# Sparse attention and a squared-ReLU layer in one kernel: the arrival of s, b, w_out and one band of v, the first fillers, and new priorities of the planner

## The chip, the cores and the metric

The kernel runs on one core of a Trainium2 chip. A core has TensorE (PE in the profile, with its weight loads as PEld), VectorE (DVE), ScalarE (ACT), GpSimd (POOL) and SyncE (SP), which issues transfers. Sixteen DMA engines move data between the memory of the chip and the core's on-chip memory. The metric is the time on the device in microseconds. Lower is better.

## The reference

Eight batches of eight heads with 576 positions and 64 channels go through attention with fixed masks, and the result goes through a layer with a squared ReLU.

```python
scores = q @ k.T / 8                                # per batch and head, 576 x 576
mask_local   = (rel >= 0) & (rel < 32)              # heads 0 to 3; rel = query - key
mask_strided = (rel >= 0) & (key % 32 == query % 32)  # heads 4 to 7
attn = softmax(where(mask, scores, -1e9)) @ v
x = attn, heads side by side                        # 4608 x 512
h = x @ w_in                                        # 512 x 2048
g = s * relu(h) ** 2 + b                            # s and b are single numbers
out = g @ w_out                                     # 2048 x 512, float32
```

## The kernel before

**Attention.** A batch is done in four pairs of heads: m = 0 and 1 are the local pairs, m = 2 and 3 the strided ones. `pair_steps` makes the steps of a pair: transposes of q and k on TensorE (line 439 for the local pairs of batches 0 and 1, line 447 for others; later batches use DMA transposes), scores (line 568, with the mask added by line 565 in batch 0), exp on ScalarE (line 586), the product with v ("av", line 629), reciprocal and multiplication (lines 646 and 656) into `x_nat`, and the transpose to `xT` (line 676). The local pairs read v from `v_loc`, which has 128 partitions: a band of 96 positions and the 32 positions before it. `rows_before` copies these 32 rows on chip after the band has landed.

**The layer.** The 4608 tokens are cut into nine blocks T of 512. F1 is x @ w_in (`ff1`, line 928; line 1153 for the last two blocks), with a ReLU on ScalarE (line 954) or VectorE (line 956) and a square. F2 is g @ w_out (`ff2`, line 1183, for blocks 0 and 1; line 896 for later ones). From block 2 on, F2 is done with seven products in place of eight, and combinations of w_out (`w_mix`) and of g are added up on VectorE. The factor s and the term b come in at the end: F2's evacuation is out = s * psum + bcs (line 1194, or lines 815 and 827), where `bcs` is b times the column sums of w_out, made once by `bcs_steps` (lines 1210, 1221, 1228).

**What sets the order.** The class `Plan` holds a clock in ns. Every step on TensorE is a `Step` with a duration, needs, perhaps a PSUM bank, and "posts": work on other engines that it sets off. The main loop at the end of the kernel emits, at each time of this clock, an attention step, an F1 step or an F2 step whose needs are met, F1 before F2. The order in which steps are emitted is the fixed order of TensorE's instructions. Landings of transfers are assumed: `landing(cost)` adds the costs of transfers in the order of their requests, from a starting point `ring`. A step is therefore placed by assumed times, and on the chip TensorE waits at it if the data come later. `Plan.flush` chooses among posted work for ScalarE and VectorE: the smallest ready time plus an allowance from the table `LATER`, by the kind of the work; `SLACK` says how far ahead of the clock an engine may be given work.

While nothing is ready and fewer than 16 F1 steps have been emitted, `keep_running` emits fillers: matmuls of ones into a free bank (line 1431). The clock starts at 1850.

**The requests.** GpSimd asks for most loads,[...] in this order: q and k of batch 0, half of its band v, its strided v; then w_in in four parts (line 339); then, by `second`, q and k of batch 1 (lines 302 and 317), its band v (`load_vl`, line 322), its strided v (`early_v`), and w_out in four parts (line 345); then batch 2. SyncE asks for the identity, the other half of batch 0's band, the masks and, at lines 1311 and 1312, for s and b, each read from one number and spread over 128 partitions by the transfer:

```python
nc.sync.dma_start(out=s_sb, in_=moe_s.to_broadcast([128, 1]))
nc.sync.dma_start(out=b_sb, in_=moe_b.to_broadcast([128, 1]))
```

Of the kernel before, what the change touches and what calls it, by code (L numbers as in the profile page):

```python
# [1 line left out]

# [1 line left out]

# [7 lines left out]
FP32 = mybir.dt.float32  # L12
# [4 lines left out]
class Plan:  # L17
# [6 lines left out]

    LAT = {"A": 70.0, "V": 70.0, "P": 70.0, "D": 12000.0, "X": 7000.0, "Y": 12000.0}

    SLACK = 800.0
    LATER = {"g": 1500.0, "S": 1500.0, "in": 2500.0, "w_mix": 2500.0, "wc": 1500.0}

    def __init__(self):  # L30
        self.t = 0.0
        self.done = {}
        self.pend = []
        self.free = {"A": 0.0, "V": 0.0, "P": 7000.0, "D": 0.0, "X": 0.0, "Y": 0.0}
        self.banks = {}
# [85 lines left out]
        self.keys, self.posts, self.after = keys, posts, after  # L121


@with_exitstack
def kernel(
    ctx: ExitStack,
# [7 lines left out]
    moe_b: bass.AP,  # L134
    out: bass.AP,
):
    nc = tc.nc
    B, H, S, D = q.shape
    NTOK, DM = out.shape
    DFF = moe_w_in.shape[1]  # L140
    stride = 32
    scale = 1.0 / float(np.sqrt(D))
    PS = 512
# [40 lines left out]
    ident = const.tile([128, 128], FP16)  # L184
    masks = const.tile([128, LQ + SQ], FP16)
    mask_loc, mask_str = masks[:, 0:LQ], masks[0:SQ, LQ:LQ + SQ]
    s_sb = const.tile([128, 1], FP32)
    b_sb = const.tile([128, 1], FP32)

    w_in_sb = [const.tile([128, 4, n], FP16, name=f"w_in_sb{i}")  # L190
               for i, n in enumerate((512, 512, 512, 512))]
# [37 lines left out]
    x_dram = [tc.dram_tile([S, 128], FP16, name=f"x_dram{i}") for i in range(4)]  # L229

    sched = ctx.enter_context(tc.manual_schedule())
    plan = Plan()

# [100 lines left out]
    def load_w_in():  # L336
        wv = moe_w_in.rearrange("(c p) f -> p c f", p=128)
        for i, at in enumerate((0, 512, 1024, 1536)):
            nc.gpsimd.dma_start(out=w_in_sb[i], in_=wv[:, :, at:at + w_in_sb[i].shape[2]])

    def load_w_out(chunks):

# [76 lines left out]
    def pair_steps(b, m):  # L419
# [135 lines left out]
        def score(i, group):  # L555

            g, n = i // per_s, min(per_s, nt - i // per_s * per_s)

            def f():
                if i % per_s == 0:  # L560
                    st["s", g] = bank(group)
                c = i % per_s * 2 * nq
                if b < PE_MASK:

                    nc.tensor.matmul(
                        out=st["s", g][0:nk, c:c + 2 * nq], lhsT=ident[0:nk, 0:nk],
                        rhs=neg_loc if loc else neg_str, start=True, stop=False)
                nc.tensor.matmul(  # L568
                    out=st["s", g][0:nk, c:c + 2 * nq], lhsT=(st["k"][:, i * nq:i * nq + nk] if loc else st["k"][:, i, 0:SQ]),
                    rhs=st["q"][:, i].rearrange("d e c -> d (e c)"), start=b >= PE_MASK, stop=True)  # L570

            s = Step(f, (2 if b < PE_MASK else 1) * (2 * nq / 2.4 + 8), needs=[("q", id_), ("k", id_)],
                     group=group if i % per_s == 0 else None)
            if i % per_s == n - 1:
                key = ("s", id_, g)
                s.keys = [key]

                ng = nt // per_s + (nt % per_s > 0)

                def ex(eng):  # L580
                    if g == 0:
                        st["whole"] = p_bufs[loc][p_taken[loc] % len(p_bufs[loc])]
                        p_taken[loc] += 1
                    at = g * 2 * per_s * nq
                    st["pw", g] = st["whole"][:, at:]
                    nc.scalar.activation(  # L586
                        out=st["pw", g][0:nk, 0:2 * n * nq],
                        in_=st["s", g][0:nk, 0:2 * n * nq], func=AF.Exp, scale=scale)

                def ms(eng):  # L590
                    pt = st["whole"][:, 0:2 * nt * nq].rearrange("k (t c) -> k t c", c=nq)
                    mask = (mask_loc if loc else mask_str)[:, None, :].to_broadcast(
                        [nk, 2 * nt, nq])
                    nc.vector.tensor_tensor(out=pt[0:nk], in0=pt[0:nk], in1=mask, op=ALU.mult)

                free = [("a", (b - 1, m), 1 if loc else 2)] if b else []
                s.posts = [([key] + free, {"A": 170 + 0.83 * 2 * n * nq}, ex,
                            [("p" if b < PE_MASK else "e", id_, g), group])]
                if b >= PE_MASK and g == ng - 1:
                    s.posts.append(([("e", id_, x) for x in range(ng)],  # L600
                                    {"V": 150 + 0.52 * 2 * nt * nq}, ms,
                                    [("p", id_, x) for x in range(ng)]))
            return s
# [626 lines left out]
        return first, second, third  # L1230


    def arrive(keys, at):
        for k in keys:
            plan.done[k] = at
# [4 lines left out]
    def landing(cost):  # L1240

        nonlocal ring
        ring = max(ring, plan.t + 2000.0) + cost

        return ring + (6000.0 if plan.t > 60000.0 else 600.0)
# [4 lines left out]
    def fetch_qk(b):  # L1250
        for mm in range(2):
            if (b - 1, "kTs", mm) in loaded:

                nc.gpsimd.tensor_copy(out=gate[0:1, 2 + mm:3 + mm],  # L1254
                                      in_=loaded[b - 1, "kTs", mm][0:1, 0, 0:1])
        load_qk(b)
        for name in ("q", "k"):
            if b >= (QB_DMA if name == "q" else KB_DMA):
                arrive(both(name + "l", b), landing(4600))
                continue  # L1260
            if b < HEAD_T:
                arrive(both(name + "l", b), landing(2400 if name == "q" else 2600))
                continue
            plan.done["raw", name, b] = landing(1700 if b > 1 else 2400 if name == "q" else 2500)
            for mm in range(2):
                pair_post(b, name, mm, ("raw", name, b))
        for name in ("qs", "ks"):
            arrive(both(name, b), landing(2000 if b > 1 else 1200))
# [39 lines left out]
    plan.done["raw", "v", False, 0] = AT["vs"]  # L1308
    after_landing(0, loaded[0, "ql"][0:1, NL // 2:NL // 2 + 1])
    nc.sync.dma_start(out=masks, in_=h_mask.ap())  # L1310
    nc.sync.dma_start(out=s_sb, in_=moe_s.to_broadcast([128, 1]))
    nc.sync.dma_start(out=b_sb, in_=moe_b.to_broadcast([128, 1]))
    def weights_in(eng):

        nonlocal ring
        nc.gpsimd.tensor_copy(out=gate[0:8, 2:3], in_=loaded[0, "qs"][64:SQ, 0:1])
        load_w_in()
        ring = 14200.0
        for keys, cost in ([0], 2700), ([1], 2500), ([2], 2500), ([3], 2500):
            arrive([("w_in", c) for c in keys], landing(cost))  # L1320

# [11 lines left out]
    def second(eng):  # L1333

        fetch_qk(1)
        load_vl(1)
        plan.done["raw", "vl", 1] = landing(2000)
        for mm in range(2):
            rows_before(1, mm, ("raw", "vl", 1))
        early_v(1)  # L1340
        weights_out(range(4))

    plan.post(both("vl", 0) + both("vs", 0) + [("w",)], {"P": 12500.0}, second, [("free",)])

# [29 lines left out]
    for T in range(NBLK):  # L1374
        if T == 0:

            gr = [Group("s", SB, "f1", F1B) for _ in range(4)]
            cts = FIRST
            f1 += [ff1(T, ft, ct, gr[ft], cts, True) for ct in cts for ft in range(4)]
        for ft in ff_order(T)[0 if T else 4:] if T < FIRST7 else ():  # L1380
            gr = Group("f1", F1B, "f2", F2B) if T == 0 else Group("f1", F1B)
            for ct in range(4):
                f1.append(ff1(T, ft, ct, gr))
        if T == FIRST7:
            f1 += ff1_seven()
        if T == 0:

            gr = [Group(*x) for x in [("f2", F2B), ("f2", F2B), ("s", SB), ("f2", F2B)]]
            sums = bcs_steps(Group("s", SB))
            for c in range(0, NFT, 4):  # L1390
                if c >= NFT - 8:
                    f2.append(sums[c // 4 - 2])
                f2 += [ff2(T, ts, ft, gr[ts]) for ts in range(2) for ft in range(c, c + 4)]
            f2.append(sums[2])
            f2 += [ff2(T, ts, ft, gr[ts]) for ts in (2, 3) for ft in range(NFT)]
            for i, s in enumerate(f2):
                s.pos = 1.25 * (i + 1) / len(f2)
            mix_post()
            continue
        if T >= SEVEN:  # L1400
            f2 += ff2_seven(T)
            continue
        for ts in range(4):

            parts = 2 if T == NBLK - 1 and ts == 3 else 1
            for part in range(parts):
                gr = Group("f2", F2B)
                for ft in range(NFT):
                    f2.append(ff2(T, ts, ft, gr, part, parts))
                    f2[-1].pos = T + 0.25 + (ts + (part + ft / NFT) / parts) / 4  # L1410
    combine_w()
    for T in range(FIRST7, NBLK):
        combine_x(T)
    plan.t = 1850.0

    def keep_running(until):

# [25 lines left out]

    def due():

        pos = f1_pos[i1] + (f2[i2 - 1].pos if i2 else 0.0) + 0.1
        return (pos if pos <= 1 else 1 + (pos - 1) / 2) * batch_ns

    while i2 < len(f2) or any(at_i[p] < len(att[p]) for p in range(len(att))):
# [40 lines left out]
    while plan.pend:  # L1490
        plan.flush()
        if plan.pend:
            plan.advance()


# [28 lines left out]
```

## Time and profile before

| | |
|---|---|
| time, median of 3 runs | 300.05 us (299.94 to 300.83) |
| the profiled execution's own time | 300.66 us |
| its span (first to last instruction) | 298.8 us |
| TensorE busy | 289.0 us, 97% |
| VectorE busy | 236.6 us, 79% |
| ScalarE busy | 191.9 us, 64% |
| GpSimd busy | 94.1 us, 32% |
| moved by DMA | 38.19 MB, 128 GB/s over the span |

Times in the profile count from the start of the span, so 1.9 us of the execution's time lie around it. Matmuls are pipelined and their ends are modelled: TensorE can be "busy" and still not work at its full rate, so the distance from one start to the next says more than busy time. "Idle before" an instruction names what ended the wait.

### The profile page before, as it was taken

The numbers are of one execution on the slowest core, as the hardware profiler recorded it, in microseconds if no ns is written. First come the engines' busy times: TensorE is split into PE (matmuls) and PEld (weight loads), VectorE is DVE, ScalarE is ACT, GpSimd is POOL, SyncE is SP. The second block draws the span as 40 slices with busy tenths as digits, with TensorE's granted clock in tenths as the row PEclk, the third lists the DMA queues.
The fourth block names the chain that finished last, engine by engine and source line by source line (L and its number), as shares of the span: only waits on it lengthen the run. The fifth ranks groups of instructions, "written<-read, shape, count | busy, mean of one in ns | idle before, by whom it ended". The sixth has DMA issues, their size and how long they took to land.

```text
span 298.8 us, 7101 instructions
## 1 busy us (share of the span) xinstructions
PE 289.0 (97%) x2800; PEld 219.2 (73%) x2800; DVE 236.6 (79%) x500; ACT 191.9 (64%) x335; POOL 94.1 (32%) x141
## 2 busy tenths in 40 slices
PE   7888989999999999999999999999999999999995
PEld 3764655666556567889866786778888989999984
DVE  6855797888886889767987798769898788888963
ACT  3575974898727797646793887378977545675400
POOL 8973343610951198007810592100010000000000
PEclk9999999999999999999999999999999999999999
DMA  8999999999999599999999999994120200210214
GB/s 133 159 204 204 176 216 190 173 192 138 120 171 166 92 114 129 136 200 109 158 155 209 125 163 155 142 176 131 43 77 20 100 29 15 70 37 1 96 49 142
DMA packets 106436, 38.19 MB, mean 128 GB/s; under 512 B 85698, under 2 KB 104258, under 8 KB 106402
## 3 DMA queue, kind: packets, MB, share of 16 engines
q0 software_dynamic: 60848, 18.23, 63.9%
q1 hardware_dynamic: 45554, 19.51, 33.9%
q8 instruction: 22, 0.36, 0.5%
q14 instruction: 12, 0.10, 0.1%
HBM read 36.99 MB, written 10.62 MB: 159 GB/s over the span
## 4 chain that ended last, share of the span: by engine, by line
PE 84%; DMA 10%; POOL 3%; ACT 1%; issue 1%; DVE 0%; POOLq 0%; ACTq 0%
PE ps_f L928 28%; PE ps_f L896 25%; PE ps_f L1183 8%; DMA kl<-in_k_dram 4%; PE ps_s L568 4%; DMA w_out_sb<-in_moe_w_out_dram 3%; PE ps_f L1153 3%; PE ps_a L629 2%; DMA vs<-in_v_dram 2%; PE ps_t L1153 2%; PE ps_a L1153 2%; PE ps_s L896 2%; PE ps_s L1153 2%; PE ps_t L629 1%; PE ps_t L896 1%; PE ps_s L1183 1%
## 5 line engine op out<-in xcount | busy, mean ns | idle before, releaser
L928 PE MATMUL ps_f<-xT,w_in_sb 128*128 128x512 f16 (+4 forms) x568 | 115.5, 331 | 0.0
L954 ACT ACTIVATE u<-ps_f 128x512 f16<-128x512 f32 x107 | 62.8, 594 | 34.2 <-PE ps_f L928 32.6
L928 PEld LDWEIGHTS <-w_in_sb 128*128 128x128 f16 x576 | 57.4, 114 | 22.7 <-DMA w_in_sb<-in_moe_w_in_dram 0.8
L896 PEld LDWEIGHTS <-gT 128*128 128x128 f16 x608 | 58.5, 98 | 9.6
L896 PE MATMUL ps_f<-w_out_sb,gT 128*128 128x256 f16 x376 | 54.9, 273 | 0.0
L1183 PE MATMUL ps_f<-w_out_sb,gT 128*128 128x512 f16 x112 | 29.4, 379 | 0.9 <-DMA w_out_sb<-in_moe_w_out_dram 0.9
L586 ACT ACTIVATE p_str<-ps_s 72x432 f16<-72x432 f32 (+1 forms) x45 | 20.5, 484 | 9.9 <-PE ps_s L568 9.5
L962 ACT ACTIVATE gT<-u 128x1024 f16<-128x1024 f16 x24 | 25.4, 1058 | 0.7
L964 DVE TENSOR_TENSOR gT<-u 128x1024 f16<-128x1024 f16 x32 | 21.8, 682 | 4.5 <-ACT u L954 4.0
L896 PE MATMUL ps_f<-w_mix,gT 128*128 128x256 f16 x176 | 24.9, 273 | 0.0
L586 ACT ACTIVATE p_loc<-ps_s 128x384 f16<-128x384 f32 x46 | 21.4, 494 | 4.7 <-PE ps_s L568 4.2
L656 DVE TENSOR_TENSOR x_nat<-ps_a,rec 96x384 f16<-96x384 f32 (+2 forms) x46 | 23.9, 519 | 0.6
L764 DVE TENSOR_TENSOR gT<-gT 128x1024 f16<-128x1024 f16 x34 | 22.6, 680 | 0.7 <-ACT gT L962 0.6
L327 POOL DMA_DIRECT2D v_loc<-in_v_dram x24 | 17.7, 744 | 7.7 <-DMA w_out_sb<-in_moe_w_out_dram 4.0
L896 PEld LDWEIGHTS <-S 128*128 128x128 f16 x176 | 17.1, 98 | 3.0
L1183 PEld LDWEIGHTS <-gT 128*128 128x128 f16 x128 | 11.5, 98 | 10.7 <-DMA w_out_sb<-in_moe_w_out_dram 1.4
L646 DVE RECIPROCAL rec<-ps_a 96x6 f32<-96x6 f32 (+2 forms) x46 | 8.4, 183 | 11.9 <-PE ps_a L629 11.8
L629 PEld LDWEIGHTS <-p_str 72*128 72x128 f16 x256 | 13.3, 98 | 5.5
L332 POOL DMA_DIRECT2D v_str<-in_v_dram x16 | 13.0, 816 | 11.3 <-PE ps_f L928 3.3
L1254 POOL COPY gate<-kT 1x1 f16<-1x1 f16 x6 | 2.5, 412 | 43.2 <-DMA kT<-ks 43.2
L896 PE MATMUL ps_f<-w_mix,S 128*128 128x256 f16 x112 | 15.7, 273 | 0.0
L1094 ACT ACTIVATE gT<-u 128x1024 f16<-128x1024 f16 x13 | 13.8, 1059 | 1.7 <-DVE u L1073 1.4
(234 smaller groups left out, 526.8 us busy)
## 6 DMA issues: line engine op xcount, KB each, us to landing
out_dram<-o SPq DMA_DIRECT2D x34, 256.0 KB, 2.3
w_in_sb<-in_moe_w_in_dram POOLq DMA_DIRECT2D x4, 512.0 KB, 11.4
w_out_sb<-in_moe_w_out_dram POOLq DMA_DIRECT2D x4, 512.0 KB, 11.5
qs<-in_q_dram POOLq DMA_DIRECT2D x6, 288.0 KB, 6.7
ks<-in_k_dram POOLq DMA_DIRECT2D x6, 288.0 KB, 9.1
v_loc<-in_v_dram POOLq DMA_DIRECT2D x24, 72.0 KB, 9.8
ql<-in_q_dram POOLq DMA_DIRECT2D x4, 288.0 KB, 10.6
kl<-in_k_dram POOLq DMA_DIRECT2D x16, 72.0 KB, 3.9
```

Source lines behind the costliest of these rows:

```text
L327: nc.gpsimd.dma_start(out=vl[LPAD:128, h, :, 0:D], in_=v_band(b, h))
L586: nc.scalar.activation(out=st["pw", g][0:nk, 0:2 * n * nq], in_=st["s", g][0:nk, 0:2 * n * nq], func=AF.Exp, scale=scale)
L629: nc.tensor.matmul(out=st["pa", g][:, n % 6, :], lhsT=st["pw", gp_][0:nk, i * nq:i * nq + WIDE], rhs=vt[0:nk, 2 * mm + e, j, :])
L656: nc.vector.tensor_tensor(out=x_at(0, cnt), in0=st["pa", g][0:nq, 0:cnt, 0:D], in1=st["rec", g][0:nq, 0:cnt].to_broadcast([nq, cnt, D]), o ...
L764: {"V": nc.vector, "P": nc.gpsimd}[eng].tensor_tensor(out=at(out), in0=at(x), in1=at(y), op=op)
L896: nc.tensor.matmul(out=gts[name, T, t][:, 0] if halves else gts[name, T][:, t], lhsT=lhs(k, t), rhs=rhs(k), start=fresh and k == 0 and (ha ...
L928: nc.tensor.matmul(out=gts["h", T, ft][:, lo:hi], lhsT=w_in_sb[ft // 4][:, ct].rearrange("p (x l) -> p l x", l=4)[:, ft % 4], rhs=xT[ct][: ...
L954: nc.scalar.activation(out=u, in_=gts["h", T, ft], func=AF.Relu)
L962: nc.scalar.activation(out=g, in_=u, func=AF.Square)
L964: nc.vector.tensor_tensor(out=g, in0=u, in1=u, op=ALU.mult)
L1153: nc.tensor.matmul(out=st[bk][:, 256 * t:256 * t + 256], lhsT=lhs(t, c), rhs=rhs(c), start=fresh and t == c == 0, stop=t == c == 1, skip_g ...
L1183: nc.tensor.matmul(out=gts[id_], lhsT=gts[T][:, ft, ts * 128:(ts + 1) * 128], rhs=w_out_sb[:, ft, cols], start=(ft == 0), stop=(ft == NFT ...
```

## The change

1. The clock of the order starts at 1050 instead of 1850, so the first fillers cover 0.8 us more of it.
2. s and b are loaded as two single numbers into one row, and a new step `sb_step` spreads them: a matmul of a row of 1/32 with this row, and a ScalarE copy times 32 into `sb_all`, of which `s_sb` and `b_sb` are now columns. The step is the first of F2's list.
3. In `second`, batch 1's band v is asked for behind w_out instead of ahead of it, and its strided v ahead of w_out as before. Its assumed cost goes from 2000 to 2600, and w_in's landings are assumed 1 us earlier.
4. The table of allowances becomes `ORDER`: 26 kinds of work instead of 5, some of them negative (sooner), with `SLACK` 600 instead of 800, and `ahead`, which says how early attention steps are due, 0.05 instead of 0.1. The kernel's body becomes `lay_out`, which can be run on objects that do nothing in order to compare tables; with `ORDERS = 0` no other table is tried.
5. In exp, the buffer is taken by the first group that comes, where it was group 0 that took it.

```diff
-    SLACK = 800.0
-    LATER = {"g": 1500.0, "S": 1500.0, "in": 2500.0, "w_mix": 2500.0, "wc": 1500.0}
+    def __init__(self, order):
+        self.SLACK, self.ahead, self.LATER = order["SLACK"], order["ahead"], order
...
+ORDER = {"g": 1500.0, "S": 2500.0, "in": 2500.0, "w_mix": 0.0, "wc": 1000.0, "ev": 1000.0,
+         "c21": 1500.0, "c11": 500.0, "c12": 500.0, "C22": -1500.0, "fv": 0.0, "Vb": -400.0,
+         "x": -1500.0, "Ub": 1000.0, "xc": -1500.0, "fe": -400.0, "k": 1500.0, "fu": -1500.0,
+         "Va": 500.0, "p": 0.0, "c22": 500.0, "Ua": 2500.0, "e": -1500.0, "q": 0.0, "r": 0.0,
+         "u": 0.0, "SLACK": 600.0, "ahead": 0.05}
...
-    s_sb = const.tile([128, 1], FP32)
-    b_sb = const.tile([128, 1], FP32)
+    sb_row = const.tile([1, 2], FP32)
+    sb_all = const.tile([128, 2], FP32)
+    s_sb, b_sb = sb_all[:, 0:1], sb_all[:, 1:2]
...
-                    if g == 0:
+                    if "whole" not in st:
...
+    def sb_step():
+        group = Group("s", SB, "f2", F2B)
+        def f():
+            gts["sb"] = bank(group)[:, 0:2]
+            nc.tensor.matmul(out=gts["sb"], lhsT=part32[0:1, :], rhs=sb_row, start=True, stop=True)
+        def g(eng):
+            nc.scalar.activation(out=sb_all, in_=gts["sb"], func=AF.Copy, scale=32.0)
+        return Step(f, 150, needs=[("sb_row",)], group=group, keys=[("sb_ps",)],
+                    posts=[([("sb_ps",)], {"A": 250.0}, g, [("sb",), group])])
...
-    nc.sync.dma_start(out=s_sb, in_=moe_s.to_broadcast([128, 1]))
-    nc.sync.dma_start(out=b_sb, in_=moe_b.to_broadcast([128, 1]))
+    nc.sync.dma_start(out=sb_row[0:1, 0:1], in_=moe_s[None, :])
+    nc.sync.dma_start(out=sb_row[0:1, 1:2], in_=moe_b[None, :])
+    plan.done["sb_row",] = 16000.0
...
-        ring = 14200.0
+        ring = 13200.0
...
     def second(eng):
         fetch_qk(1)
+        early_v(1)
+        weights_out(range(4))
         load_vl(1)
-        plan.done["raw", "vl", 1] = landing(2000)
+        plan.done["raw", "vl", 1] = landing(2600)
         for mm in range(2):
             rows_before(1, mm, ("raw", "vl", 1))
-        early_v(1)
-        weights_out(range(4))
...
+            f2.append(sb_step())
...
-    plan.t = 1850.0
+    plan.t = 1050.0
...
-        pos = f1_pos[i1] + (f2[i2 - 1].pos if i2 else 0.0) + 0.1
+        pos = f1_pos[i1] + (f2[i2 - 1].pos if i2 else 0.0) + plan.ahead
```

More of the change, by code (lines that the diff above doesn't have):

```diff
@@ L1 @@
 from contextlib import ExitStack
+import random
 import numpy as np
@@ L25 @@
     LAT = {"A": 70.0, "V": 70.0, "P": 70.0, "D": 12000.0, "X": 7000.0, "Y": 12000.0}
-    SLACK = 800.0
-    LATER = {"g": 1500.0, "S": 1500.0, "in": 2500.0, "w_mix": 2500.0, "wc": 1500.0}
-    def __init__(self):
+    def __init__(self, order):
         self.t = 0.0
+        self.SLACK, self.ahead, self.LATER = order["SLACK"], order["ahead"], order
         self.done = {}
@@ L121, in __init__, with varied, __getattr__, __call__ @@
         self.keys, self.posts, self.after = keys, posts, after
+ORDER = {"g": 1500.0, "S": 2500.0, "in": 2500.0, "w_mix": 0.0, "wc": 1000.0, "ev": 1000.0,
[3 rows of a table added]
+         "u": 0.0, "SLACK": 600.0, "ahead": 0.05}
+KINDS = ("g", "S", "in", "w_mix", "wc", "Va", "Ua", "Ub", "Vb", "C22", "xc", "q", "k", "r", "x", "e",
+         "p", "u", "ev", "fv", "fu", "fe", "c11", "c22", "c21", "c12")
+def varied(order, rnd):
+    order = dict(order)
+    for kind in rnd.sample(KINDS, rnd.choice((1, 2, 4))):
+        order[kind] = rnd.choice((-1500.0, -800.0, -400.0, 0.0, 500.0, 1000.0, 1500.0, 2500.0))
+    if rnd.random() < 0.2:
+        order["SLACK"] = rnd.choice((400.0, 600.0, 800.0, 1000.0))
+    if rnd.random() < 0.2:
+        order["ahead"] = rnd.choice((0.0, 0.05, 0.1, 0.2))
+    return order
+class Nothing:
+    def __getattr__(self, name):
+        if name.startswith("__"):
+            raise AttributeError(name)
+        return self
+    def __call__(self, *args, **kw):
+        return self
+    def __getitem__(self, at):
+        return self
+ORDERS = 0
 @with_exitstack
@@ L136, with lay_out @@
 ):
[L137 to L140, printed above, removed]
+    shapes = q.shape, out.shape, moe_w_in.shape
+    nothing = [Nothing()] * 11
+    rnd = random.Random(0)
+    best = ORDER
+    end = lay_out(*nothing, best, *shapes)
+    for _ in range(ORDERS):
+        other = varied(best, rnd)
+        at = lay_out(*nothing, other, *shapes)
+        if at < end:
+            best, end = other, at
+    lay_out(ctx, tc, tc.nc, q, k, v, moe_w_in, moe_w_out, moe_s, moe_b, out, best, *shapes)
+def lay_out(ctx, tc, nc, q, k, v, moe_w_in, moe_w_out, moe_s, moe_b, out, order, q_shape, out_shape,
+            w_in_shape):
+    B, H, S, D = q_shape
+    NTOK, DM = out_shape
+    DFF = w_in_shape[1]
     stride = 32
@@ L231 @@
     sched = ctx.enter_context(tc.manual_schedule())
-    plan = Plan()
+    plan = Plan(order)
     NL, NS = 4 * LT * D, 4 * ST * D
@@ L338, in load_w_in @@
         for i, at in enumerate((0, 512, 1024, 1536)):
-            nc.gpsimd.dma_start(out=w_in_sb[i], in_=wv[:, :, at:at + w_in_sb[i].shape[2]])
+            nc.gpsimd.dma_start(out=w_in_sb[i], in_=wv[:, :, at:at + 512])
     def load_w_out(chunks):
@@ L1493 @@
             plan.advance()
+    return plan.t
 _INS = ['q', 'k', 'v', 'moe_w_in', 'moe_w_out', 'moe_s', 'moe_b']
```

## The prediction

> **What bounds the kernel now.** I read the engines' busy times and the slices first, then TensorE's own waits, then the chain that ended last cut to the first 42 us, then the windows around two of its steps. Page and waits:
>
> ```profile
> PE 289.0 (97%) x2800; PEld 219.2 (73%) x2800; DVE 236.6 (79%) x500; ACT 191.9 (64%) x335; POOL 94.1 (32%) x141
> ...
> PE   7888989999999999999999999999999999999995
> ...
> GB/s 133 159 204 204 176 216 190 173 192 138 120 171 166 92 114 129 136 200 109 158 155 209 125 163 155 142 176 131 43 77 20 100 29 15 70 37 1 96 49 142
> ```
>
> TensorE is full from the sixth or seventh slice (7.47 us each) to the end. Busy time includes the modelled ends of matmuls, so I also took the starts of consecutive matmuls in the trace and subtracted columns / 2.4 GHz. What is left over is 1.5 us between 50 us and the last matmul, and most of that is three gaps of 0.2, 0.25 and 0.44 us at 177, 207 and 241 us. So after 50 us the time is work, which the change does not cut; before it, TensorE waits for transfers, and the transfers run at about 200 GB/s without a break. The early part of the timeline of TensorE, DMA rows from the chain:
>
> ```profile
> 1.06 3.26 PE L1431 MATMUL ps_s<-w_mix 128*128 128x512 f16 x9 [1.06 <-DVE w_mix L261]
> 5.38 0.45 PE L439 MATMUL ps_t<-ident,ql 96*64 96x96 f16 x12 [1.07 <-DMA ql<-in_q_dram]
> ...
> 18.64 0.41 PE L928 MATMUL ps_s<-xT,w_in_sb 128*128 128x512 f16 x1 [0.60 <-DMA w_in_sb<-in_moe_w_in_dram]
> ...
> 28.82 0.45 PE L439 MATMUL ps_t<-ident,ql 96*64 96x96 f16 x12 [0.77 <-DMA ql<-in_q_dram]
> ...
> 40.66 0.61 PE L1183 MATMUL ps_f<-w_out_sb,gT 128*128 128x512 f16 x2 [0.91 <-DMA w_out_sb<-in_moe_w_out_dram]
> ```
>
> ```profile
> 7.85 6.47 DMA vs<-in_v_dram
> ...
> 17.36 13.17 DMA kl<-in_k_dram
> ...
> 30.81 9.80 DMA w_out_sb<-in_moe_w_out_dram
> ```
>
> Three waits behind data, at 18.64, 28.82 and 40.66 us. A matmul's modelled end hides about 0.17 us of each, so from start to start they cost 0.76, 0.94 and 1.07 us: **2.8 us in all**. These are what the change can take. Around 20 us there are another 0.6 us for an x_nat on VectorE and 0.3 us of fillers, and at 14.5 us 0.6 us for kTs on VectorE.
>
> Why is w_in late? The windows (TensorE, its weight loads, VectorE, ScalarE, GpSimd, clock, DMA share, GB/s):
>
> ```profile
> 12.00:13.00 1.00, 1.00 (x24) 1.00 (x22) 0.95 (x3) 1.00 (x6) 1.00 (x2) 1.00 1.18 190
> 13.00:14.00 1.00, 1.00 (x25) 0.87 (x21) 0.99 (x3) 1.00 (x4) 0.96 (x2) 1.00 0.40 48
> 14.00:15.00 1.00, 0.58 (x11) 0.46 (x10) 0.82 (x2) 0.65 (x2) 0.70 (x2) 1.00 0.52 99
> 15.00:16.00 1.00, 1.00 (x25) 1.00 (x22) 0.64 (x3) 0.65 (x2) 1.00 (x3) 1.00 1.16 189
> ```
>
> There is a hole in the transfers: 48 and 99 GB/s where its neighbours have 190. All four w_in transfers had been asked for by 13.4 us, so there was work. By packet, what runs in the hole are the 256 packets of 4 bytes of the s and b broadcasts (lines 1311 and 1312): from 13.4 to 14.7 us about 75 of them per us and almost nothing else. Missing against 200 GB/s: (200 - 48) + (200 - 99) = 253 kB, **1.27 us**.
>
> **The change, part by part.**
>
> *Fillers from 1.05 us.* The order's clock starts 0.8 us earlier, which adds about two fillers of 512 columns. Fillers start 0.43 us apart until 3.8 us, so at most 0.86 us. Between the ninth filler and the first transpose of ql there are 1.07 us idle. Cost 0; without that idle time it would be 0.86 us. Nothing behind them is earlier, as ql lands when it did.
>
> *s and b.* Two requests of one packet each replace two of 128. The SP queue still issues two (0.65 us each, rows L1311 and L1312 of its timeline), with only zeros for ks behind them. Added: a small float32 matmul and a ScalarE copy. For the matmul the nearest row is L1221's, two passes of float32 in 1.02 us less 0.85 us of streaming: 0.2 us; the copy is below the 0.64 us of a 128x576 copy. Both fall into the wait before 18.64 us; 0.2 us if that is gone. The gain is the hole, and here the Trainium skill speaks against the row: DMA: Bandwidth & Descriptors, section Queues, rings and completion order, has each of the 16 engines take turns between queues by packet, and its section Bandwidth puts a small packet at some 10.5 ns. By that, an estimate: 256 x 10.5 / 16 = 0.17 us, and w_in would come at 18.4. The row shows one small packet per 13 ns for all engines together and the others standing still. I take the row, 1.3 us, and keep 0.2 as the low end. From w_in to the last of batch 1, landings follow each other without a break, so all of them move by 1.3: w_in 18.59 to 17.3, ql of batch 1 28.77 to 27.5.
>
> What TensorE makes of it: the 0.76 us before 18.64 goes, but the 0.9 us at 20 us hang on VectorE and on banks that attention still holds, so at 21 us it is ahead by some 0.5 (0 to 1.2). F1 then runs without a gap to 28.05 - 0.5 = 27.55, and ql lands at 27.5: that wait goes too. Ahead by then: **1.3 us**, set by the landing.
>
> *Band v of batch 1 behind w_out.* In the semaphore events v_loc lands at 36.76, 3.1 us after the ks ahead of it (it is the transfer of 128-byte rows), and the four w_out at 40.62, 42.38, 44.85 and 47.35. Without it ahead, w_out comes 3.1 us earlier, and 1.3 more by the hole: 36.2, 38.0, 40.4, 42.9; v_loc then lands at 46.1 instead of 36.8, and batch 2's ql behind it gains only the 1.3. Eight GpSimd transfers share eight semaphores, so each request waits for the landing of the eighth before it. The first w_out then waits for ql (27.5) instead of kl (30.53 in the chain): 9 us ahead of its landing, so the queue doesn't run dry. The requests themselves (1.19 us for v_loc, 0.53 to 0.57 for a w_out) keep their sum. TensorE gets to w_out at 39.6 - 1.3 - 0.4 (the 12 + 12 av matmuls of batch 1's local heads, which now come later) = 37.9, after it landed: the 1.07 us go. Late next is v_loc: av of the local heads at 46.8 instead of 38, x of batch 1 at about 51. Until then there are 64 x 0.216 = 13.8 us of F2, about 2 of the sums and 2.6 of strided attention: 18.4 us, to 56. The price if this cover were missing is every us by which 51 becomes later than 56.
>
> *Priorities, SLACK 600, ahead 0.05.* No operation is added. They can take at most the 0.9 us of three gaps after 170 us and part of the 1.5 us at 14 to 21 us; they can cost what the rival below says. The chain has ScalarE's exp at 175.79 and 206.28 (0.94 us each), and exp is now put ahead; I take 0.2 gained, range -3.5 to +1.5. The evacuations that end the kernel (3.5 us from the last matmul) stay.
>
> Sum: 1.3 + 1.07 + 0.2 - 0.2 (the added matmul, exposed) = 2.4. The profiled execution took 300.66 with a span of 298.8; 2.4 less gives 298.3 there. The median of the runs, 300.05, is 0.6 below that execution, so **297.7 us**.
>
> **Rivals.**
>
> *The order runs ahead of the data (298.9).* TensorE's order is fixed by assumed arrivals: w_out at 35.1 on the order's clock (38.1 before), w_in at 16.5 (17.5 before). Landings were 2.5 and 1.1 us later than assumed. If the list puts w_out or ql too early, TensorE stands in front of it while F1 work lies behind. For it: that is what the waits at 28.82 and 40.66 look like. Against: with the hole gone, the first gap is 36.2 - 35.1 = 1.1 us, and the delay at ql (27.5 against 26.4) has already put TensorE 1.1 us behind the list. If half of it returns, 1.2 of the 2.4 us are lost.
>
> *s and b do not make the hole (299.1).* Then w_in stays at 18.59 and only w_out's wait goes: 300.05 - 1.07 = 299.0, less or more 0.2. For it: the page's rule, and eight packets of zeros for ks in the same hole. Against: zeros are sent again at 38 to 40 us, at 221 and 242 GB/s.
>
> *Slower (301.4): late evacuations hold the banks.* F2 has two banks from the third block on. Ua, Va and ev now stand 2500, 500 and 1000 ns back in VectorE's choice; VectorE is busy 18.15 of 20 us in 240 to 260. A product is 16 matmuls of 0.109 us, 1.7 us, some 3.5 with F1 between; an evacuation that comes later than that stops TensorE. Seven blocks with 0.54 us each would be 3.8 us: 297.7 + 3.8 = 301.4. It decides from 0.34 us per block (2.4 / 7). Against: the list counts these releases, and before VectorE mostly waited for TensorE there, not the other way.
>
> **How the numbers follow.** Likeliest case 0.56, 297.7, own range 296.6 to 298.7. Order ahead of the data 0.17 at 298.9; hole not from s and b 0.13 at 299.1; slower 0.14 at 301.4. About 0.3% (0.9 us) is what runs of this kernel can tell from no change. Under 299.15: 0.55 of the first, 0.11 of the second, 0.07 of the third: 0.73. Over 300.95: 0.12 of the last and little else: 0.12. The rest 0.15. The range leaves out 0.05 below 296.4 and 0.14 above 300.6.
>
> **What would show it.** Right: no window under 150 GB/s between 12 and 16 us; first w_in matmul by 18.0; transposes of batch 1's ql at 27 to 28; first w_out matmul at 37 to 38.5 with no wait on w_out; the local av of batch 1 after 46; the same 1 to 2 us of gaps after 50 us. Wrong: a hole still there; a wait of over 0.5 us on ql or w_out; waits of PE on VectorE or on a bank after 100 us that add up to over 1 us.

## The result and the profile after

The changed kernel takes **298.49 us** (median of 22 runs, 297.73 to 301.1) and the kernel before 300.25 (22 runs beside it, 299.52 to 301.68). The ratio is **0.9949, 95% interval 0.9934 to 0.9964**: half a per cent faster. The profiled execution took 298.86 us with a span of 297.1, against 300.66 and 298.8 before.

TensorE's row of the busy times, and the windows around the old hole (TensorE, its weight loads, VectorE, ScalarE, GpSimd, clock, DMA share, GB/s), after:

```profile
PE 290.5 (98%) x2802; PEld 220.0 (74%) x2802; DVE 235.3 (79%) x501; ACT 194.3 (65%) x336; POOL 93.7 (32%) x140
```

```profile
12.00:13.00 1.00, 1.00 (x25) 1.00 (x23) 0.95 (x3) 1.00 (x6) 1.00 (x2) 1.00 1.32 199
13.00:14.00 1.00, 0.94 (x24) 0.78 (x20) 0.96 (x4) 1.00 (x4) 0.96 (x2) 1.00 1.14 176
14.00:15.00 1.00, 0.53 (x11) 0.53 (x12) 0.78 (x2) 0.65 (x2) 0.41 (x2) 1.00 1.24 198
15.00:16.00 1.00, 1.00 (x25) 1.00 (x22) 0.72 (x3) 0.73 (x2) 1.00 (x3) 1.00 1.24 206
```

TensorE is as full as before, 98% of a shorter span. The hole is gone: 176 and 198 GB/s where there were 48 and 99. The landings that follow it, from the semaphore events: w_in 17.10 us (before 18.59), ql of batch 1 26.41 (28.77), the four w_out 34.91, 37.64, 39.82 and 42.79 (40.62 to 47.35), v_loc of batch 1 45.35 (36.76).

TensorE's waits after, and from its timeline the places where it stood before w_in, ql and w_out, and the local av of batch 1:

```profile
PE ps_s L1502 <- DVE w_mix L316: 1.1, 1, 1.1
PE ps_f L623 <- DVE kTs L404: 0.5, 1, 0.5
PE ps_s L623 <- ACT p_loc L641: 0.4, 1, 0.4
PE ps_f L983 <- ACT u L1009: 0.3, 1, 0.3
PE ps_f L684 <- ACT p_str L641: 0.3, 1, 0.3
PE ps_a L1208 <- ACT E L404: 0.2, 1, 0.2
```

```profile
18.96 0.38 PE L983 MATMUL ps_s<-xT,w_in_sb 128*128 128x512 f16 x1
...
26.81 0.36 PE L494 MATMUL ps_t<-ident,ql 96*64 96x96 f16 x8
...
38.13 0.59 PE L1238 MATMUL ps_f<-w_out_sb,gT 128*128 128x512 f16 x2
...
46.85 0.35 PE L684 MATMUL ps_a<-v_loc,p_loc 128*128 128x65 f16 x6
```

No transfer is left in the list of waits, and none of the four rows has an idle time before it. To see when the time was gained I took, for both traces, the time that has passed less the useful streaming that TensorE has started by then (columns / 2.4 GHz plus 2.5 ns for each matmul that is not a filler; in the traces matmuls of 512 columns start 0.216 us apart). The useful work is 282.90 us in both; the rest is time lost:

```
lost by (us)     14     21.5    28     30     42     60     160    end
before          8.32   10.80  11.07  11.37  12.31  10.28  10.81  12.02
after           8.31   10.27  10.00   9.90  10.02   8.00   8.52  10.40
ahead           0.01    0.53   1.07   1.47   2.29   2.28   2.29   1.62
```

At 42 us the changed kernel is 2.29 ahead and keeps that until after 160 us. At the end it is 1.62 ahead: **0.67 us were given back between 175 and 245 us**. The waits behind VectorE or ScalarE there, after:

```profile
196.66 1.02 PE L983 MATMUL ps_f<-xT,w_in_sb 128*128 128x512 f16 x4 [0.35 <-ACT u L1009]
200.61 0.32 PE L623 MATMUL ps_s<-qD_loc,kT_alt 128*128 128x192 f16 x2 [0.42 <-ACT p_loc L641]
239.71 0.60 PE L1208 MATMUL ps_a<-xT,v_str 128*128 128x256 f16 x4 [0.24 <-ACT E L404]
```

From start to start the first two cost 0.51 and 0.58 us. The third is there in both kernels.

### The profile page after: what moved, and what is told of

The parts are those of the page before. It is cut to its first block, busy times and chain, and to the rows that moved or that the text cites. A ratio compares the mean times of both kernels' runs of the same rounds, so it can differ in the third digit from the quotient of the medians.

```text
span 297.1 us, 7092 instructions
## 1 busy us (share of the span) xinstructions
PE 290.5 (98%) x2802; PEld 220.0 (74%) x2802; DVE 235.3 (79%) x501; ACT 194.3 (65%) x336; POOL 93.7 (32%) x140
## 4 chain that ended last, share of the span: by engine, by line
PE 88%; DMA 6%; ACT 2%; DVE 2%; POOL 1%; issue 1%; ACTq 0%
PE ps_f L983 28%; PE ps_f L951 22%; PE ps_f L1238 8%; DMA v_loc<-in_v_dram 6%; PE ps_s L623 5%; PE ps_f L1208 3%; PE ps_a L684 3%; PE ps_s L1502 2%; PE ps_a L1208 2%; PE ps_s L951 2%; PE ps_t L1208 2%; PE ps_s L1208 2%; PE ps_t L951 1%; PE ps_s L1238 1%; PE ps_t L684 1%; PE ps_t L502 1%
## 5 line engine op out<-in xcount | busy, mean ns | idle before, releaser
L1009 ACT ACTIVATE u<-ps_f 128x512 f16<-128x512 f32 x104 | 61.0, 594 | 32.5 <-PE ps_f L983 31.8
L951 PE MATMUL ps_f<-w_out_sb,gT 128*128 128x256 f16 x376 | 55.6, 273 | 0.0
L1017 ACT ACTIVATE gT<-u 128x1024 f16<-128x1024 f16 x29 | 30.7, 1057 | 0.8
L1238 PE MATMUL ps_f<-w_out_sb,gT 128*128 128x512 f16 x112 | 30.4, 379 | 0.0
L1019 DVE TENSOR_TENSOR gT<-u 128x1024 f16<-128x1024 f16 x27 | 18.5, 686 | 5.9 <-ACT u L1009 5.4
L951 PEld LDWEIGHTS <-S 128*128 128x128 f16 x176 | 17.1, 98 | 2.9
L1323 POOL COPY gate<-kT 1x1 f16<-1x1 f16 x6 | 1.5, 256 | 45.0 <-DMA kT<-ks 45.0
L1149 ACT ACTIVATE gT<-u 128x1024 f16<-128x1024 f16 x12 | 12.7, 1058 | 1.7 <-DVE u L1128 1.4
```

The source lines that it names most:

```text
L951: nc.tensor.matmul(out=gts[name, T, t][:, 0] if halves else gts[name, T][:, t], lhsT=lhs(k, t), rhs=rhs(k), start=fresh and k == 0 and (ha ...
L1009: nc.scalar.activation(out=u, in_=gts["h", T, ft], func=AF.Relu)
L1017: nc.scalar.activation(out=g, in_=u, func=AF.Square)
L1019: nc.vector.tensor_tensor(out=g, in0=u, in1=u, op=ALU.mult)
L1238: nc.tensor.matmul(out=gts[id_], lhsT=gts[T][:, ft, ts * 128:(ts + 1) * 128], rhs=w_out_sb[:, ft, cols], start=(ft == 0), stop=(ft == NFT ...
```

## The experiments

My theory: the time comes from two transfers, the hole (1.3 us) and w_out (1.07), and the rest of the change is worth nothing. The rivals were that the order of work is what counts (new priorities, arrivals assumed), that the clock's early grant is what the fillers buy, and that small packets, not the broadcasts' single address, make the hole. Ratios are to the kernel before, run on the same chip. Where two ratios are subtracted, their half-widths are added as squares.

### One part alone, on the kernel before

```diff
 e1_sb:     + sb_row, sb_step and the loads of s and b, as in the change (ring stays 14200)
 e2_order:  + early_v(1); weights_out(range(4)) ahead of load_vl(1), landing(2600) (ring stays 14200)
 e4_prio:   + the table ORDER with SLACK 600 and ahead 0.05; "whole" taken by the first group
 e5_fill:   - plan.t = 1850.0
            + plan.t = 1050.0
```

> The kernel before with s and b spread on chip, nothing else. Theory (the broadcasts make the hole): no window from 13 to 15 us under 150 GB/s, first w_out landing 1.3 us or more earlier than 40.62; but the list still assumes w_in at 17.5, and w_out follows the 128-byte band, so TensorE gains 0.5 us at 21 us, 1.3 at 30 us and about 1.3 in all: ratio 0.996. Rival (something else makes the hole): a window under 100 GB/s is still there, w_in at 18.6, time within 0.2 us of before.

Measured: 301.87 us, ratio 1.004 (1.002 to 1.006). **A miss, by more than 2 us.** The hole is gone in its windows (191, 187, 185 and 195 GB/s), w_in lands at 17.23 and ql at 27.26, and still the kernel is slower.

> The kernel before with the band v of batch 1 asked for behind w_out, nothing else. Theory: the hole stays, w_in at 18.6, the waits at 18.6 and 28.8 us stay, w_out lands at 37.5 and its wait of 1.07 us is gone: 1.0 us faster, ratio 0.9965. Rival (the band is then missing, or the list stands before w_out too early): a wait on v_loc or w_out of 0.5 us or more between 36 and 55 us, and at most 0.5 us gained.

Measured: 301.1 us, 1.001 (0.999 to 1.003). A miss too: w_out lands at 37.60, TensorE does not wait for it, and nothing is gained.

> The kernel before with the new priorities, SLACK 600 and ahead 0.05, nothing else. Theory: nothing gained before 60 us, 0.7 us lost after 170 us: ratio 1.002. Rival (late gaps come from being early): gaps after 170 us as before, 1.2 us, ratio 1.000. Second rival (the priorities make part of the early gain): 0.5 us or more ahead at 60 us.

Measured: 302.6 us (6 runs), 1.0069 (1.0048 to 1.009). By themselves the new priorities cost more than either theory said. In its trace the loss is late. Three of its waits:

```profile
201.46 0.27 PE L900 MATMUL ps_f<-w_out_sb,gT 128*128 128x256 f16 x1 [0.29 <-DVE o L831]
...
205.39 0.57 PE L572 MATMUL ps_s<-qD_str,kT 128*72 128x144 f16 x6 [0.43 <-DMA kT<-ks]
...
233.62 0.49 PE L1157 MATMUL ps_s<-qD_loc,ks 128*128 128x256 f16 x3 [0.65 <-DVE qD_loc L1032]
```

The first, for the evacuation `o` that frees a bank, is of the kind of the prediction's slower rival. It is the smallest of the three, 0.46 us from start to start; the last, for a combination of x that VectorE makes into a reused buffer, costs 0.81. It loses 2.96 us between 160 us and its last matmul, where before loses 1.21. At 60 us it is 0.62 us ahead of before, past the 0.5 of the second rival; but e5 below, with before's order but for the first fillers, is 0.65 ahead there, so this mark decides nothing.

> The kernel before with the order's clock starting at 1050: more fillers at the start, nothing else. First theory, as predicted: no gain, the fillers only fill idle time: ratio 1.000, within 0.3 us. New theory, after the runs of single parts (there TensorE's granted clock rose at 9.4 to 10.1 us, in the profile before at 3.84, and the runs were 1 us behind at 14 us): the idle 1.07 us after the old fillers lets the clock rise late in a part of the executions, the new fillers do not: clock granted by 7.5 us, 0.3 to 0.8 us faster than before in the median, ratio 0.998.

Measured: 300.53 us, 0.9999 (0.9987 to 1.0012). The fillers alone are worth nothing, and the theory of the clock's early grant falls as far as this kernel goes. What a late clock costs the run does not say: in both profiles the full clock came early, at 3.8 us (before) and 4.4 us (e5).

So none of these four parts gains alone, and two of them lose; the assumed landings of w_in, moved by 1 us, were not run alone. But a part alone is not what it seems: the planner lays out the whole order again when a step or an assumed arrival changes. The timeline of e1's TensorE shows what its new order brought, at a place that the hole does not touch:

```profile
55.18 0.23 PE L448 MATMUL ps_f<-ident,ks 72*128 72x72 f16 x2 [0.23 <-DVE kT_loc L350]
...
56.01 0.42 PE L448 MATMUL ps_t<-ident,ks 72*128 72x72 f16 x8 [0.24 <-DVE qD_str L350]
```

From start to start e1 loses 0.98 us in three gaps at 54 to 57 us, and another 1.7 in two gaps at 202 and 205 us. A third loss in this trace lies ahead of these gaps: the full clock came at 9.4 us, and by 14 us e1 had lost 9.28 us where before had lost 8.32. The traces of e2 and e4 show the same (clock at 10.1 and 10.0 us, 9.27 and 9.23 us lost). The next run keeps this order and adds the early fillers.

```diff
 e11_sbfill: e1_sb with
 - plan.t = 1850.0
 + plan.t = 1050.0
```

> The kernel before with s and b spread on chip and the fillers' clock at 1050, all else old. s and b alone gave 301.87, 1.3 us over the kernel before, and its profile had the clock granted at 9.4 us. If that loss is the late clock, the early fillers take it away and the hole's 1.3 us are gained: 299.3. If it is the order of work that the new step brought about (gaps at 55 and at 200 us), which the fillers do not touch, it stays at 301.5 to 302.

Measured: 300.44 us, 1.0016 (0.9989 to 1.0044), between the two expectations, with an interval that overlaps e1's. In its trace TensorE is 1.64 us ahead of before at 42 us, so the hole's gain is there; at 60 us it is 0.69 ahead, and the gaps at 54 to 57 us (0.39, 0.41, 0.18) are what took it. Its clock came at 7.0 us and by 14 us it had lost 8.33, as before had, so about 1 us of the difference to e1 is the late clock in these two traces. Whether that holds for the 1.4 us between the two medians is not settled: the two ratios differ by 0.24%, give or take 0.34.

### One part taken out of the changed kernel

```diff
 e3_oldprio: the old five allowances, SLACK 800 and ahead 0.1 in ORDER
 e6_nofill:  - plan.t = 1050.0
             + plan.t = 1850.0
```

> The changed kernel with the five old priorities, SLACK 800 and ahead 0.1. Theory (the late gaps are the new priorities' doing): the early gain of 2.3 us stays, the gaps after 170 us go back from 1.9 us to about 1.2, so 0.7 us faster than the changed kernel: ratio to before 0.992. Rival (the late gaps come because TensorE is 2.3 us earlier and runs into ScalarE whatever the priorities): gaps after 170 us of 1.7 us or more, ratio 0.995. Second rival (the priorities made the early gain): TensorE less than 1.5 us ahead of before at 60 us.

Measured: 299.24 us, 0.9956 (0.9945 to 0.9968). Expected 0.992, so the theory falls. The ratio is that of the first rival, and so is the trace, which loses 2.4 us after 170 us: late gaps come with the old priorities too. The mark of the second rival is met as well: TensorE is 1.22 us ahead of before at 60 us (the changed kernel 2.28); ql lands at 27.77 us (26.41), and TensorE waits 0.5 us for it. One trace does not settle whether that is the priorities' doing, as before and e5 differ by 0.65 us there. By the times, the interval of the changed kernel itself overlaps: with the transfers changed, the new priorities make at most a small difference (0.2 us, give or take 0.6); on the old transfers (e4) they cost 0.7%.

> The changed kernel with the order's clock starting at 1850 again: the old fillers, nothing else. First theory: 298.5, as the changed kernel. New theory (the clock rises late without the new fillers): 0.4 to 1.0 us slower than the changed kernel in the median, ratio to before 0.997, and the profile, where its clock is granted after 8 us, about 1 us behind the changed one at 14 us.

Measured: 299.31 us, 0.9957 (0.994 to 0.9973), which again overlaps the changed kernel's 0.9949. The clock came at 4.8 us without the new fillers, so the new theory falls. The order after the first fillers is the same, but its profiled execution (298.05 us) lacks the two gaps at 197 and 201 us: it loses 1.09 us after 160 us, the changed kernel's loses 1.88.

### The order held fixed, the transfers put back

These tell most. Every instruction of the compute engines stays where the changed kernel has it; only transfers differ.

```diff
 e7_bcast: (two broadcasts that nobody reads, beside the new loads)
 + sb_un = const.tile([128, 2], FP32)
 + nc.sync.dma_start(out=sb_un[:, 0:1], in_=moe_s.to_broadcast([128, 1]))
 + nc.sync.dma_start(out=sb_un[:, 1:2], in_=moe_b.to_broadcast([128, 1]))
 e9_vahead:
 + load_vl(1)
   early_v(1)
   weights_out(range(4))
 - load_vl(1)
 e10_list: e7_bcast and e9_vahead together
```

> The changed kernel with two more loads that nothing reads: s and b spread over 128 partitions by the transfer, asked for where they were before. Theory: the hole is back, a window under 120 GB/s between 13 and 15 us, w_in at 18.4 instead of 17.1, ql of batch 1 and w_out 1.3 us later, and as the list is laid out for the early landings TensorE waits for ql by about 1 us: 0.8 to 1.3 us slower than the changed kernel, ratio to before 0.998. Rival: no hole, ratio 0.995.

Measured: 299.9 us, 0.9991 (0.9975 to 1.0007). Against the changed kernel that is 0.42% (give or take 0.22), **1.3 us**. Its windows and its wait:

```profile
12.00:13.00 1.00, 1.00 (x25) 1.00 (x23) 0.96 (x3) 1.00 (x6) 1.00 (x2) 1.00 1.30 171
13.00:14.00 1.00, 0.91 (x23) 0.74 (x19) 0.95 (x4) 1.00 (x4) 0.96 (x2) 1.00 0.70 83
14.00:15.00 1.00, 0.57 (x12) 0.57 (x13) 0.74 (x2) 0.62 (x3) 0.14 (x1) 1.00 0.51 52
15.00:16.00 1.00, 1.00 (x24) 1.00 (x21) 0.76 (x4) 0.75 (x2) 0.94 (x2) 1.00 1.22 213
```

```profile
PE ps_t L495 <- DMA ql<-in_q_dram: 1.1, 1, 1.1
```

The hole is back, ql lands at 27.88 instead of 26.41, and TensorE, which reaches it at 26.8, waits 1.1 us. That is the prediction's chain from the broadcasts to ql.

> The changed kernel with one thing put back: band v of batch 1 is requested ahead of w_out again; the order of every engine's work stays the changed one. In the changed kernel w_out landed at 34.91 and TensorE came to it at 38.13 us. Band v took 3.1 us of transfer, so w_out should land at about 38.0 and still be there in time; the next three at 40.7, 42.9 and 45.9, each about when it is needed (16 matmuls of 0.216 us, 3.5 us, apart). My theory: with the hole of s and b gone the request order by itself is worth 0 to 0.3 us, 298.5 to 298.8 us in all. Rival, the prediction's own sum: the request order is what takes the wait for w_out, so 1.07 us come back, 299.6.

Measured: 299.69 us, 0.9987 (0.9972 to 1.0002): 0.38% (give or take 0.21) over the changed kernel, **1.1 us**. My theory of that moment, that the request order is worth nothing by itself, falls; the prediction's 1.07 fits. But the wait is not the one that the prediction named. TensorE's and VectorE's timelines:

```profile
39.52 0.59 PE L1238 MATMUL ps_f<-w_out_sb,gT 128*128 128x512 f16 x2 [1.21 <-DVE u L1011]
```

```profile
36.22 0.50 DVE L404 COPY v_str<-vs 72x512 f16<-72x512 f16 x2 [1.76 <-DMA vs<-in_v_dram]
...
38.79 0.68 DVE L1011 TENSOR_SCALAR u<-ps_f 128x512 f16<-128x512 f32 x1
```

Band v goes past batch 1's strided v (vs) as well as past w_out. VectorE, in the changed order, copies vs at 34.48 us; here it stands 1.76 us before it, and behind it stands the evacuation u that frees F2's bank: 37.08 in the changed kernel, 38.79 here. w_out lands at 39.14, also 1.0 after TensorE's 38.13, so it would have stopped TensorE by nearly as much. The experiment moves band v past both and cannot price them apart.

> The changed kernel's order of work, fed by the old transfers: two unused broadcasts of s and b make the hole again, and band v is requested ahead of w_out. w_out should land at 36.3 + 3.1 = 39.4 us, with TensorE, late from ql by 1.1, there at 39.2. My theory: the loss is that of the hole and little else, 298.5 + 1.3 + 0.2 = 300.0, which is the time of the kernel before: the new order by itself gives nothing. Rival: each transfer part has its own price, 1.3 + 1.07, so 300.9; other rival: the new order is worth something by itself, 299.3 or less.

Measured: 301.58 us (10 runs), 1.0051 (1.0025 to 1.0077): 1.02% (give or take 0.3) over the changed kernel, 3.1 us. The rival with two prices is nearest; 2.4 is their sum, and the interval of 2.2 to 4.0 holds it. The traces say the same: by 42 us the changed kernel has lost 10.02 us, e7 11.13, e9 11.39 and e10 13.07, so that the hole is worth 1.1, band v's place 1.4 and both together 3.05; none of the three has the gaps at 197 and 201 us. The two waits stand side by side:

```profile
PE ps_f L1239 <- DVE u L1012: 1.3, 1, 1.3
PE ps_t L495 <- DMA ql<-in_q_dram: 1.3, 1, 1.3
```

This is also the new order on the old transfers, and it is **slower than the kernel before**. The new order is worth something only with the data that it was laid out for.

### Is it the size of the packets, or their address?

```diff
 e8_distinct: (instead of e7's broadcasts: as many packets of 4 bytes, 256 addresses)
 + for i in range(2):
 +     nc.sync.dma_start(out=sb_un[:, i:i + 1],
 +                       in_=moe_w_in[i:i + 1, 0:128].rearrange("o p -> p o"))
```

> The changed kernel with two more loads that nothing reads: 128 neighbouring numbers of w_in each, one to a partition, so again 256 packets of 4 bytes, but from different addresses. If it is the one address that all packets read which makes the engines stand still: no window under 150 GB/s, w_in at 17.1 to 17.3, time of the changed kernel. If it is the small packets as such: the same hole as with the broadcasts, w_in at 18.4.

Measured: 298.98 us (seven executions; an eighth took 611 us), 0.9953 (0.9938 to 0.9968), like the changed kernel. The profiled execution is the one of 611 us (the last section says what its trace shows) and serves for its transfers alone. They do not side with the time: w_in landed at 18.14 us, near the 18.4 of small packets as such and not at 17.1 to 17.3, and one window had 135 GB/s, under my limit of 150. The next run is the same kernel, for a profile of usual length.

> The same kernel as the one with 256 packets of 4 bytes read from 256 different addresses, once more for a profile with the clock granted. If the hole comes from packets of one address, no stretch of 1 us between 12 and 16 us is under 130 GB/s and ql of batch 1 lands by 27.2 us; if it comes from small packets as such, two stretches are under 100 GB/s, as with the broadcasts (83 and 52), and ql lands at 27.9.

Measured: 299.32 us, 0.9959 (0.9945 to 0.9974). Its windows:

```profile
12.00:13.00 1.00, 1.00 (x25) 1.00 (x23) 0.96 (x3) 1.00 (x6) 1.00 (x3) 1.00 1.46 126
13.00:14.00 1.00, 0.91 (x23) 0.74 (x19) 0.95 (x4) 1.00 (x4) 0.53 (x1) 1.00 1.49 161
14.00:15.00 1.00, 0.57 (x12) 0.57 (x13) 0.74 (x2) 0.61 (x3) 0.72 (x1) 1.00 0.99 156
15.00:16.00 1.00, 1.00 (x24) 1.00 (x21) 0.76 (x4) 0.75 (x2) 0.16 (x1) 1.00 1.25 204
```

A dip, no hole: the DMA engines stay busy (shares of 1.46, 1.49, 0.99, where the broadcasts have 0.70 and 0.51 in the last two). Missing against the changed kernel's windows from 12 to 16 us are 132 kB, 0.66 us at 200 GB/s; with the broadcasts (e7) it is 260 kB, 1.3 us. Both of my limits were missed by a little: one window has 126 GB/s, not 130, and ql lands at 27.32, not by 27.2. In this trace TensorE has lost 0.55 us more than the changed kernel by 42 us, in e7's 1.11. So the traces put about half of the loss on the packets as such. The medians of the two runs put them at 0.1 to 0.3 us, against 1.3 for the same packets from one address each, but each of these figures is good to 0.6 us only. The windows show a dip with distinct addresses and a hole with one; how the 1.3 us divide between the packets and their address is not settled. The distinct packets also come from another array, which no run separates from the address.

## Why the prediction was right, and by how much it missed

It said 297.7 us, range 296.4 to 300.6, and 298.49 was measured.

- **The hole, 1.3 us: right.** e7 gives 1.3 by the times, give or take 0.66, and 1.1 by its trace; that s and b do not make the hole is refuted. Two details of the working were not right. At most 127 of the 256 small packets started between 13.4 and 14.7 us; the others ran before, mostly from 12.6 to 13.4. And the page did not speak against the row: DMA: Bandwidth & Descriptors, section Bandwidth, of the Trainium skill gets its 10.5 ns by dividing the 0.67 us of a whole transfer by that transfer's 64 packets, so I should not have divided by 16 engines once more, and the 0.17 us do not follow from it. Undivided it gives, as an estimate, 2.7 us for 256 packets. Neither figure fits either of the two cases that were run (0.3 to 0.66 us of bandwidth from distinct addresses, 1.3 from one address each); the row of the trace was the better guide.
- **Landings: right in direction, too small.** ql moved by 2.36 us instead of 1.3 and w_out by 5.7 instead of 4.4. About 1 us more came between w_in and ql; e7, with the hole, still has ql 0.9 earlier than before. It need not lie in the new order: profiles with the same requests differ by half a microsecond in ql (28.77 and 28.33 in before and e5, 27.26 and 26.72 in e1 and e11). Its cause is open. As ql was early, its transposes began at 26.81, ahead of the 27 to 28 that I had given.
- **TensorE's lead: right, but the tenths are luck.** Predicted 0.5 at 21 us, 1.3 near 28, 2.4 near 42; shown 0.53 at 21.5, 1.07 at 28 and 1.47 at 30, 2.29 at 42. That holds for one pair of profiles: against the profile of e5, which has before's order but for the first fillers, the lead at 42 us is 1.66.
- **w_out, 1.07 us: right in size, half right in mechanism.** 1.1 by e9, give or take 0.6. The first w_out matmul was at 38.13 us with no wait, as predicted for 37 to 38.5. But in the new order VectorE's copy of vs comes before w_out, and I had not listed it among what is queued behind band v; band v's place decided about vs too.
- **Late band v: right.** The local av of batch 1 began at 46.85 us, after 45.35, without a wait: F2 covered it.
- **The order runs ahead of the data: did not happen with the new transfers,** because they came as assumed: w_out at 34.91 against an assumed 35.1. It is what e10 shows when the transfers are put back.
- **Fillers, 0: right.** The extra fillers of 512 columns ran 0.43 us apart and, with those behind them, pushed the first transposes of kl from 6.71 to 7.17; by 14 us both kernels have lost the same (8.32 and 8.31).
- **The sb matmul, 0.2 at most: right.** At 16.34 us it adds gaps of 0.13, 0.13 and 0.17 us. The marker "first w_in matmul by 18.0" was wrong: it began at 18.96, not for w_in's sake (landed at 17.10) but because the new order puts more attention first.
- **Priorities, 0.2 gained: the term that was mis-sized.** In the two profiles the late part costs 0.67 us more than before. The two gaps that do it, at 197 and 201 us, stand in two of six profiles with this order (the changed kernel and e12, and not in e6, e7, e9, e10), so they are not a fixed price of the priorities; what sets them off is open. With the new transfers the priorities are worth nothing that can be measured (e3); I should have given them 0, with the range downward. From 50 us on the changed kernel's profile loses 2.4 us by the measure of the table (before 1.8), more than the 1 to 2 that I had named as a sign of being right.

The working: from profile to profile 2.4 us were predicted and 1.80 came (300.66 to 298.86). The front gave 2.29 against 1.3 + 1.07 - 0.2 = 2.17; the late part took 0.67 where it was to give 0.2; what follows the last matmul's start is 0.18 shorter. 0.12 - 0.87 + 0.18 is -0.57, which is the difference. The other 0.2 us of the miss are the median of before, 300.25 over 22 runs where three had 300.05.

What stays open: why e1 and e2 have medians as high as they have. Their traces show where their orders lose (gaps at 54 to 57, 84, and 202 to 205 us) and that both had their full clock late, which cost 1 us by 14 us (in e2 that is hidden by 30 us, where it and before have both waited for ql); the runs with a fixed order show that the transfers do have their price. That the new order eats what the transfers give is argued from one trace each. The run nearest to the old order with the new transfers is e3, and it keeps 0.44% of the 0.51.

## What to carry to other kernels

Where each engine's order is fixed ahead of time, an edit to a transfer does two things: it moves the data, and it makes the planner lay out another order. Price them apart by holding the order and putting the transfer back (an unused copy of it will do): here that gave 1.3 and 1.1 us where the same edits made alone gave a loss of 0.4% and nothing. When a request is moved, list every transfer that it passes and the first instruction on each engine that needs one of them.

## What the runs showed of the hardware

Two transfers of 128 packets of 4 bytes that each read one address came with a pause in all transfers that cost about 1.3 us of bandwidth (48 and 99 GB/s before, 83 and 52 in e7, in place of about 190). The DMA engines' share fell from 1.2 or 1.3 to 0.4 to 0.7 meanwhile: for much of the time they had no packet in flight, rather than being busy with small ones. The same number of packets from different addresses took 0.3 (e8) to 0.66 us (e12) of the bandwidth and left no such pause.

TensorE's full clock came at 3.8 (before), 6.4 (after), 7.0 (e11), 9.4 (e1) and 10.1 us (e2) after the span's start. The distance from one filler of 512 columns to the next shows it (0.43 us, then 0.22), while the clock column of the windows says 1.00 throughout. In the two late traces TensorE had lost 1 us more by 14 us than in the others. In one execution of e8 such matmuls stayed about 0.44 us apart to the end, half the rate of the changed kernel's 0.216, and the kernel took 611 us.
